# Longer latencies for five kinds of transfer in the planner of an attention and two-MLP kernel

## The chip, the core and the metric

The kernel runs on one core of a Trainium2 chip. A core has five engines that each run their own instructions in order: TensorE (PE in the profile, with PEld for its weight loads), VectorE (DVE), ScalarE (ACT), GpSimd (POOL) and SyncE (SP). SP and POOL issue the DMA transfers here. The metric is the device time of one execution in microseconds.

## The reference

Attention within chunks of 64 positions, for 8 batches, 8 heads, 576 positions and a head size of 64; its output, as 4608 tokens of 512 values, goes through two MLPs.

```python
# attention, for each chunk of 64 positions
scores = (q_c @ k_c.T) / 8.0
scores = scores - scores.max(-1)
attn = exp(scores); attn = attn / (attn.sum(-1) + 1e-9)
x = (attn @ v_c)                    # 4608 x 512
# first MLP: 512 -> 2048 -> 512
h = x @ w_in
g = maximum(h, 0) + log1p(exp(-abs(h)))
x = g @ w_out
# second MLP: 512 -> 768 -> 512
h = maximum(maximum(x @ w1, x @ w2), x @ w3)
out = h @ w_out2
```

The weights of both MLPs arrive as 64-bit floats (pairs of 32-bit words).

## The kernel before

The 4608 tokens are cut into nine blocks of 512. The first MLP's blocks 0 to 2 are multiplied plainly (L717 for x @ w_in, L737 for g @ w_out, twelve MATMULs each). Blocks 3 to 8 use a scheme with seven products of quarter matrices in place of eight: `UnitA` takes two column blocks of w_in at a time in products p1 to p7, each of six MATMULs of L1102, and `mlp1_out` (L1176) is the output step of twelve MATMULs. The second MLP does the same with `Unit2` and `Unit` (L1279, L970) and `mlp2_out` (L1387). Every f32 operand is held as a high and a low part, so each product needs three passes.

Beside the first MLP run three kinds of work that feed later stages.

- `attention(t)`: for each of 28 tiles, q, k and v are loaded into the single buffers rq, rk and rv (`loads`; L428 and L453 are the transfers), DVE transposes q and k (L623, L624), PE forms scores and the products with v of an older tile in one step (L486, tile aps), DVE and ACT do the softmax (L521 to L528), DVE transposes the result (L663), and it goes through memory and back (pd<-s at L667, s<-pd at L672).
- `early(n)`: 24 raw weights of the second MLP are loaded by POOL (L303, L308), converted from 64-bit words in six DVE steps that begin at L317 (`conv`), and stored by SP as w2d (L779) or wo2d (L774). Only one of them is under way at a time (the place kind "early").
- POOL reads prepared first-MLP weights back in each unit (s<-wac and s<-wae, L1039).

After a product PE's result in ph is copied into a tmp by ACT (`keep`, L266) or added to one by DVE (`add`, L273), and the softplus (L1124) and the cut into parts (g) follow; later products and the output step wait for those. There are nine tmps. At the end of a block `finish` copies four results from acc into tmps, and SP stores them to x2d (L705).

The order on every engine is made by `Plan.order`, before anything runs. Each operation has a cost per engine, and a latency `lat` (time behind its cost until its result can be used) or, for transfers, a `move` that occupies a modelled queue. Due times are passed back from each operation to those it depends on, less cost and latency. The planner then steps through modelled time and, on each idle engine, starts the ready operation that is due first; an operation is ready when all it depends on has ended, and the buffers that it allocates must be free. The result is one list in order of modelled start; each engine takes its own rows from it, in that order. On the chip an engine waits with semaphores wherever the modelled time was too short, and everything behind it on that engine waits too.

Of the kernel before, what the change touches and what calls it, by code (L numbers as in the profile page):

```python
# [10 lines left out]
F32 = mybir.dt.float32  # L11
# [17 lines left out]
def f32_of_bits(x):  # L29
    return float(np.array([x], np.uint32).view(np.float32)[0])  # L30
# [27 lines left out]
class Plan:  # L58
# [6 lines left out]
    def op(self, engs, fn, r=(), w=(), alloc=(), hold=(), after=(), due=None, lat=0.0, move=0.0):  # L65
        o = Op()
        o.move = move
        o.follow = o.start = None
        o.engs, o.fn, o.due, o.lat, o.allocs = engs, fn, due, lat, list(alloc)
        deps = dict.fromkeys(after)  # L70
        bufs = dict.fromkeys(o.allocs + list(hold))
        for item in r:
            b, key = item if isinstance(item, tuple) else (item, None)
            deps.update(dict.fromkeys(b.writers[key] if key in b.writers and key is not None else sum(b.writers.values(), [])))
            bufs[b] = None
        for item in w:
            b, key = item if isinstance(item, tuple) else (item, None)
            if key is None:
                deps.update(dict.fromkeys(sum(b.writers.values(), []) + sum(b.readers.values(), [])))
            else:  # L80
                deps.update(dict.fromkeys(b.writers.get(key, []) + b.readers.get(key, []) + b.readers.get(None, [])))
            bufs[b] = None
        for item in r:
            b, key = item if isinstance(item, tuple) else (item, None)
            b.readers.setdefault(key, []).append(o)
        for item in w:
            b, key = item if isinstance(item, tuple) else (item, None)
            b.writers[key] = [o]
        for b in bufs:
            if b.first is None:  # L90
                b.first = o
            else:
                deps[b.first] = None
        o.deps = list(deps)
        o.bufs = list(bufs)
        for b in o.bufs:
            b.uses += 1
        o.n = len(self.ops)
        self.ops.append(o)
        return o  # L100
# [79 lines left out]
def tile_kernel(ctx: ExitStack, tc: tile.TileContext, q, k, v, w_in, w_out, w1, w2, w3, wo2, out):  # L180
    nc = tc.nc
    B, H, S, D = q.shape
# [55 lines left out]
    wo2d = [dram.tile([P, 2, TB], F32, name=f"wo2d{j}") for j in range(NJ2)]  # L238
    w2d = [dram.tile([P, TB], F32, name=f"w2d{n}") for n in range(3 * NJ2)]
# [12 lines left out]
    def slot(*kinds, shape=[P, 2, TB], dt=F32R):  # L252
        return Buf(*kinds, fresh=lambda i: slot_at(i, shape, dt))
# [5 lines left out]
    op = plan.op  # L259
# [20 lines left out]
    NP = 3  # L280
# [9 lines left out]
    def in_line(kind, o):  # L290
        o.follow, line[kind] = line.get(kind), o
        return o


    def conv(src, view, kinds, due=None, after=(), most=("load",), rest=None, first=None, by="S"):

        raw, a, t, free = slot(*kinds, shape=[P, TB, 2], dt=I32), Buf("tmp"), Buf("tmp"), Buf(*most)
        kind, j = view

        def load(e):  # L300
            start = (nc.gpsimd if e == "G" else nc.sync).dma_start
            if kind == "in":
                start(  # L303
                    out=raw.t.rearrange("p (k f) t -> p k (f t)", k=KD),
                    in_=src[:, j * 2 * P:(j + 1) * 2 * P].rearrange("(k p) f -> p k f", p=P),
                )
            else:
                start(out=raw.t.rearrange("p f t -> p (f t)"), in_=src[j * P:(j + 1) * P, :])  # L308

        in_line("load", op({by: 0.5}, load, w=[raw], alloc=[free, raw], after=after, lat=2.0, move=2.2, due=first))  # L310
        hw = lambda: raw.t[:, :, 1]
        lw = lambda: raw.t[:, :, 0]
        ai = lambda: a.t.bitcast(I32)
        ti = lambda: t.t.bitcast(I32)
        op(
            {"D": 0.43},
            lambda e: nc.vector.tensor_scalar(ai(), hw(), 0x7FFFFFFF, None, ALU.bitwise_and),  # L317
            r=[raw],
            w=[a],
            alloc=[a, t],  # L320
        )
        op(
            {"D": 0.43},
            lambda e: nc.vector.tensor_scalar(
                a.t, a.t, f32_of_bits(0x47EFFFFF), f32_of_bits(0x38000000), ALU.min, ALU.max
            ),
            w=[a],
        )
        op(
            {"D": 0.43},  # L330
            lambda e: nc.vector.tensor_scalar(ai(), ai(), 3, 0x3FFFFFF8, ALU.logical_shift_left, ALU.bitwise_and),
            w=[a],
        )
        op(
            {"D": 0.69},
            lambda e: nc.vector.scalar_tensor_tensor(
                ai(), hw(), -0x40000000, ai(), ALU.bitwise_and, ALU.bitwise_or
            ),
            r=[raw],
            w=[a],  # L340
        )
        op({"D": 0.43}, lambda e: nc.vector.tensor_scalar(ti(), ai(), -0x800000, None, ALU.bitwise_and), r=[a], w=[t])
        last = op(
            {"D": 0.69},
            lambda e: nc.vector.scalar_tensor_tensor(
                rest.t[:, 1] if rest else t.t, lw().bitcast(U32), 2.0**-52, t.t, ALU.mult, ALU.mult
            ),
            r=[raw, t],
            w=[(rest, "rest")] if rest else [t],
            alloc=[rest] if rest else [],  # L350
            hold=[free],
            due=due,
        )
        return a, t, last
# [105 lines left out]
    def loads(fns, buf, key, move, alloc=(), engs="S", after=(), due=None):  # L460
        fns = list(fns)
        if alloc:
            op({engs: 0.0}, lambda e: None, alloc=alloc, after=after)
        for n, fn in enumerate(fns):
            op(
                {e: 0.5 if due is not None else 0.65 for e in engs},
                lambda e, fn=fn: fn({"A": nc.scalar, "S": nc.sync, "G": nc.gpsimd}[e].dma_start),
                w=[(buf, (key, n))],
                after=after,
                lat=5.0 if due is None else 1.8,  # L470
                move=move / len(fns),
                due=due,
            )
# [211 lines left out]
    def finish(b, to, due, h):  # L685

        acc = acc_of[b]
        for m in range(KD):
            o = Buf("tmp")
            src = lambda m=m: acc[m // 2].t[:, m % 2]  # L690
            if (b, m) in store:
                op(
                    {"S": 0.48},
                    lambda e, o=o, m=m: nc.sync.dma_start(out=o.t, in_=partd[b][:, m, :]),
                    w=[o],
                    alloc=[o],
                    after=[store[b, m], h],
                    lat=2.2,
                    due=due,
                )  # L700
                tt_op(lambda o=o: o.t, src, lambda o=o: o.t, ALU.add, [acc[m // 2]], [o], due=due + 4 * STEP)
            else:
                copy_op(lambda o=o: o.t, src, [acc[m // 2]], [o], psum=True, alloc=[o], due=due + 4 * STEP)
            store[b, m] = op(
                {"S": 0.48}, lambda e, o=o, m=m, to=to: nc.sync.dma_start(out=to[b][:, m, :], in_=o.t), r=[o], lat=2.5, move=1.0  # L705
            )

    def mlp1(b, j, first, last):
# [44 lines left out]
        if last:  # L753
            finish(b, partd if j < NJ - 1 else x2d, T0 + STEP * s, h)
# [5 lines left out]
    store = {}  # L760
# [7 lines left out]
    def early(n, due, after):  # L768

        if n < NJ2:  # L770
            a, t, _ = conv(wo2, ("out", n), ("x", "z"), after=after, most=("early",), by="G")
            z = slot("x", "z")
            cut_up(z, lambda: a.t, [a], alloc=[z], rest=t, due=due)
            store["o", n] = op({"S": 0.48}, lambda e: nc.sync.dma_start(out=wo2d[n], in_=z.t.bitcast(F32)), r=[z], lat=2.0, move=2.2)  # L774
            return
        n -= NJ2
        a, t, _ = conv((w1, w2, w3)[n // 2 % 3], ("in", n // 6 * 2 + n % 2), ("x", "z"), after=after, most=("early",), by="G")
        tt_op(lambda: a.t, lambda: a.t, lambda: t.t, ALU.add, [t], [a], due=due)
        store["w", n] = op({"S": 0.48}, lambda e: nc.sync.dma_start(out=w2d[n], in_=a.t), r=[a], lat=2.0, move=1.1)  # L779

    rings, first_ws = [], []

# [697 lines left out]
    for n, f in enumerate((1.0, -1.0)):  # L1480
        op(
            {"D": 0.2},
            lambda e, n=n, f=f: nc.vector.tensor_scalar(eye.t[:, n, :P], ident, f, None, ALU.mult),
            w=[(eye, n)],
            alloc=[] if n else [eye],
            after=[made],
            due=-9.0,
# [60 lines left out]
```

## Time and profile before

| | us |
|---|---|
| median of 3 runs (1430.91 to 1434.74) | 1431.5 |
| the profiled execution, its own time | 1433.25 |
| its span, first to last instruction | 1431.5 |
| PE busy | 1394.8 (97%) |
| DVE busy | 883.0 (62%) |
| ACT busy | 507.1 (35%) |
| POOL busy | 266.4 (19%) |
| mean granted TensorE clock | 0.991 |

How to read the rows further below. A table of stretches has, for each, its bounds and length, then the busy time of each engine with its instructions in brackets, the granted clock of TensorE as a share of full speed, the share of time that the DMA engines were busy, and GB/s. A timeline row has the start and length of some equal instructions that follow each other, engine, line, operation, written tile <- read tiles, shapes and count, and in square brackets the time that the engine had idled just before and what ended it. The table of waits has who waited for what: total us, number of waits, the longest. The chain of work is followed back from the last instruction; its rows have start, length and what it was. Rows of DMA issues have written <- read tile, issuing queue, count, size of one, and the median us from issue to landing. The list that orders the engines counts steps: one step of PE is a product (six MATMULs), an output step (twelve) or an attention step (64).

### The profile page before, as it was taken

The numbers are of one execution on the slowest core, as the hardware profiler recorded it, in microseconds if no ns is written. First come the engines' busy times: TensorE is split into PE (matmuls) and PEld (weight loads), VectorE is DVE, ScalarE is ACT, GpSimd is POOL, SyncE is SP. The second block draws the span as 40 slices with busy tenths as digits, with TensorE's granted clock in tenths as the row PEclk, the third lists the DMA queues.
The fourth block names the chain that finished last, engine by engine and source line by source line (L and its number), as shares of the span: only waits on it lengthen the run. The fifth ranks groups of instructions, "written<-read, shape, count | busy, mean of one in ns | idle before, by whom it ended". The sixth has DMA issues, their size and how long they took to land.

```text
span 1431.5 us, 25706 instructions
## 1 busy us (share of the span) xinstructions
PE 1394.8 (97%) x9994; PEld 1194.9 (83%) x9994; DVE 883.0 (62%) x1676; ACT 507.1 (35%) x1000; POOL 266.4 (19%) x471
## 2 busy tenths in 40 slices
PE   5999999999999999999999999999999999999998
PEld 4788878888898888888888998888888888888897
DVE  7978866858777676667664466757345444544423
ACT  3533233334344333343432445523223222322212
POOL 1000112322323323323232011111011011101300
PEclk8999999999999999999999999999999999999999
DMA  8553455775968949867476374755434533624720
GB/s 252 165 153 110 136 180 160 228 256 160 296 195 243 294 132 298 249 192 249 148 258 222 133 269 174 278 199 191 146 126 161 193 132 124 222 74 169 302 103 30
DMA packets 232474, 272.00 MB, mean 190 GB/s; under 512 B 143456, under 2 KB 163296, under 8 KB 232352
## 3 DMA queue, kind: packets, MB, share of 16 engines
q0 software_dynamic: 49472, 169.64, 33.6%
q1 hardware_dynamic: 182064, 99.93, 24.7%
q8 instruction: 79, 1.29, 0.4%
q10 hardware_dynamic: 816, 0.79, 0.2%
q14 instruction: 43, 0.35, 0.1%
HBM read 208.14 MB, written 62.13 MB: 189 GB/s over the span
## 4 chain that ended last, share of the span: by engine, by line
PE 85%; DMA 8%; DVE 3%; issue 2%; POOL 1%; SPq 1%; ACT 1%; ACTq 0%; POOLq 0%
PE ph L1279 14%; PE acc L1176 12%; PE ph L1102 12%; PE acc L1387 10%; PE one L1279 10%; PE ph L717 9%; PE acc L737 9%; DMA s<-in_moe_w_dram 2%; PE aps L486 2%; PE ph L970 2%; DMA pd<-s 2%; PE one L970 1%; PE acc L486 1%; DMA rq<-in_q_dram 1%; DMA s<-pd 1%
## 5 line engine op out<-in xcount | busy, mean ns | idle before, releaser
L1176 PE MATMUL acc<-g,s 128*128 128x512 f32 x1152 | 281.3, 393 | 0.2 <-DVE g L273 0.2
L1102 PE MATMUL ph<-s,s 128*128 128x256 f32 x2016 | 264.8, 285 | 14.4 <-DVE tmp L273 6.2
L1102 PEld LDWEIGHTS ph<-s,s 128*128 128x128 f32 x2016 | 256.6, 192 | 26.5 <-DVE tmp L273 7.6
L266 ACT COPY tmp<-ph 128x256 f32<-128x256 f32 (+1 forms) x277 | 124.9, 451 | 350.9 <-PE ph L1279 211.1
L1176 PEld LDWEIGHTS acc<-g,s 128*128 128x128 f32 x1152 | 211.9, 190 | 40.8 <-DVE g L273 0.5
L1279 PE MATMUL ph<-s,s 128*128 128x512 f32 x864 | 212.6, 389 | 0.0
L273 DVE TENSOR_TENSOR tmp<-one,tmp 128x512 f32<-128x512 f32 (+1 forms) x122 | 77.1, 632 | 211.7 <-PE one L1279 173.3
L1279 PEld LDWEIGHTS ph<-s,s 128*128 128x128 f32 x864 | 162.2, 188 | 33.6
L273 DVE TENSOR_TENSOR g<-tmp,g 128x512 fp32r<-128x512 f32 x168 | 115.3, 686 | 77.7 <-ACT g L266 77.2
L453 POOL DMA_DIRECT2D rv<-in_v_dram x152 | 93.1, 618 | 361.6 <-PE aps L486 280.4
L1279 PE MATMUL one<-s,s 128*128 128x512 f32 x648 | 158.8, 389 | 0.0
L1279 PEld LDWEIGHTS one<-s,s 128*128 128x128 f32 x648 | 121.5, 188 | 25.0
L717 PE MATMUL ph<-s,s 128*128 128x512 f32 x576 | 140.1, 393 | 0.3 <-DVE s L273 0.3
L737 PE MATMUL acc<-g,s 128*128 128x512 f32 x576 | 140.0, 392 | 0.0
L273 DVE TENSOR_TENSOR tmp<-ph,tmp 128x256 f32<-128x256 f32 (+1 forms) x172 | 76.1, 454 | 86.2 <-PE ph L1102 85.6
L717 PEld LDWEIGHTS ph<-s,s 128*128 128x128 f32 x576 | 108.7, 190 | 23.7 <-DVE s L273 0.8
L737 PEld LDWEIGHTS acc<-g,s 128*128 128x128 f32 x576 | 107.1, 188 | 22.8 <-DVE g L273 0.3
L844 POOL DMA_DIRECT2D s<-w2c x96 | 51.0, 533 | 353.4 <-PE one L1279 139.2
L266 ACT CAST g<-tmp 128x512 fp32r<-128x512 f32 x161 | 100.4, 624 | 45.7 <-PE acc L737 25.6
L1124 ACT ACTIVATE tmp<-tmp 128x256 f32<-128x256 f32 x96 | 50.4, 525 | 163.5 <-DVE tmp L273 163.5
L266 ACT CAST s<-tmp 128x512 fp32r<-128x512 f32 (+1 forms) x122 | 72.0, 599 | 48.6 <-DVE tmp L273 33.1
L1039 POOL DMA_DIRECT2D s<-wac x108 | 58.4, 542 | 158.9 <-PE ph L1102 115.4
(131 smaller groups left out, 1504.5 us busy)
## 6 DMA issues: line engine op xcount, KB each, us to landing
s<-wac POOLq DMA_DIRECT2D x108, 512.0 KB, 6.4
s<-w2c POOLq DMA_DIRECT2D x96, 512.0 KB, 4.6
w2c<-s POOLq DMA_DIRECT2D x24, 512.0 KB, 4.1
wac<-s POOLq DMA_DIRECT2D x18, 512.0 KB, 4.8
x2d<-tmp SPq DMA_DIRECT2D x36, 256.0 KB, 4.2
s<-wae POOLq DMA_DIRECT2D x18, 512.0 KB, 5.7
s<-in_moe_w_dram POOLq DMA_DIRECT2D x18, 512.0 KB, 5.8
s<-in_moe_w_in_dram SPq DMA_DIRECT2D x16, 512.0 KB, 4.4
```

The lines of the kernel that those rows point to most:

```text
L266: nc.scalar.copy(dst(), src())
L273: return op({"D": 0.69 * n}, lambda e: nc.vector.tensor_tensor(dst(), a(), b(), f), r=r, w=w, **kw)
L453: dma(out=dst().rearrange("p (c e d) -> p c e d", e=2, d=D)[half * CH:(half + 1) * CH, lo:lo + mine, h, :], in_=v[b, t % HP * 2 + h].rearr ...
L717: nc.tensor.matmul(ph.t, w[:, wi, kk * P:(kk + 1) * P], x[kk].t[:, xi], start=(kk == 0 and wi == 0 and xi == 0), stop=(kk == KD - 1 and wi ...
L737: nc.tensor.matmul(acc[m // 2].t[:, m % 2], w[:, wi, m * P:(m + 1) * P], g.t[:, gi, :], start=(first and wi == 0 and gi == 0), stop=(last ...
L844: lambda e, k=k, z=z, w=w: nc.gpsimd.dma_start(out=z.t[:, :, w].bitcast(F32), in_=(w2e[n // 2] if k == 3 else w2c[n][k])[:, :, w]),
L1039: lambda e, k=k: nc.gpsimd.dma_start(out=new[k].t.bitcast(F32), in_=wac[n][k] if k < 3 else wae[n // 2]),
L1102: nc.tensor.matmul(z.t[:, half * HT:(half + 1) * HT], ws.t[:, wi, col + kk * P:col + (kk + 1) * P], x.t[:, xi, kk * HT:(kk + 1) * HT], sta ...
L1124: in_line("y", op({"A": n}, lambda e: nc.scalar.activation(to(), src(), AF.Softplus), r=r, w=w))
L1176: nc.tensor.matmul(acc[m // 2].t[:, m % 2], w.t[:, wi, m * P:(m + 1) * P], g.t[:, gi, :], start=(first and wi == 0 and gi == 0), stop=(las ...
L1279: nc.tensor.matmul(dst(), ws.t[:, wi, col + kk * P:col + (kk + 1) * P], x[kk].t[:, xi], start=(first and kk == 0 and wi == 0 and xi == 0), ...
L1387: nc.tensor.matmul(acc[t // 2].t[:, t % 2], g.t[:, gi, t * P:(t + 1) * P], wo.t[:, wi], start=(j == 0 and wi == 0 and gi == 0), stop=(j == ...
```

## The change

Five latencies in the planner get larger; nothing that an instruction computes is touched. Raw weights that POOL loads count 9.0 in place of 2.0, the loads of q, k and v without a due time of their own (those of tiles from the second block on) 9.0 in place of 5.0, the stores of x2d at the ends of the first MLP's blocks 3 to 8 7.0 in place of 2.5, and the stores of converted weights 6.0 and 7.0 in place of 2.0.

```diff
-        in_line("load", op({by: 0.5}, load, w=[raw], alloc=[free, raw], after=after, lat=2.0, move=2.2, due=first))
+        in_line("load", op({by: 0.5}, load, w=[raw], alloc=[free, raw], after=after, lat=9.0 if by == "G" else 2.0, move=2.2, due=first))
...
-                lat=5.0 if due is None else 1.8,
+                lat=9.0 if due is None else 1.8,
...
-                {"S": 0.48}, lambda e, o=o, m=m, to=to: nc.sync.dma_start(out=to[b][:, m, :], in_=o.t), r=[o], lat=2.5, move=1.0
+                {"S": 0.48}, lambda e, o=o, m=m, to=to: nc.sync.dma_start(out=to[b][:, m, :], in_=o.t), r=[o], lat=7.0 if b >= NP else 2.5, move=1.0
...
-            store["o", n] = op({"S": 0.48}, lambda e: nc.sync.dma_start(out=wo2d[n], in_=z.t.bitcast(F32)), r=[z], lat=2.0, move=2.2)
+            store["o", n] = op({"S": 0.48}, lambda e: nc.sync.dma_start(out=wo2d[n], in_=z.t.bitcast(F32)), r=[z], lat=6.0, move=2.2)
...
-        store["w", n] = op({"S": 0.48}, lambda e: nc.sync.dma_start(out=w2d[n], in_=a.t), r=[a], lat=2.0, move=1.1)
+        store["w", n] = op({"S": 0.48}, lambda e: nc.sync.dma_start(out=w2d[n], in_=a.t), r=[a], lat=7.0, move=1.1)
```

The list that the planner makes of it differs on all engines but PE, where 984 of 991 steps keep their index and the others move by one or two. Three places.

**First piece: DVE in block 6, around one raw weight's conversion** (tile s43 before, s35 now; L317 is its first step, and the rows that read ph0 or ph1 are additions on PE's products). Before:

```order
L273 TENSOR_TENSOR g2_74<-tmp2_77,g2_74 128x512
L317 TENSOR_SCALAR tmp6_81<-s43_314_7291 128x512
L324 TENSOR_SCALAR tmp6_81<-tmp6_81 128x512
L331 TENSOR_SCALAR tmp6_81<-tmp6_81 128x512
L273 TENSOR_TENSOR tmp4_79<-ph1_90,tmp4_79 128x256
L336 SCALAR_TENSOR_TENSOR tmp6_81<-s43_314_7291,tmp6_81 128x512
L342 TENSOR_SCALAR tmp0_75<-tmp6_81 128x512
L345 SCALAR_TENSOR_TENSOR tmp0_75<-s43_314_7291,tmp0_75 128x512
L273 TENSOR_TENSOR tmp6_81<-tmp6_81,tmp0_75 128x512
L273 TENSOR_TENSOR g0_72<-tmp4_79,g0_72 128x512
L273 TENSOR_TENSOR tmp5_80<-ph1_90,tmp5_80 128x256
```

And now:

```order
L273 TENSOR_TENSOR g2_74<-tmp5_80,g2_74 128x512
L273 TENSOR_TENSOR tmp2_77<-ph1_90,tmp2_77 128x256
L273 TENSOR_TENSOR g0_72<-tmp2_77,g0_72 128x512
L273 TENSOR_TENSOR tmp0_75<-ph1_90,tmp0_75 128x256
L623 STREAM_TRANSPOSE s41_319_7428<-rq0_71 128x512
L317 TENSOR_SCALAR tmp4_79<-s35_316_7327 128x512
L273 TENSOR_TENSOR tmp8_83<-ph1_90,tmp8_83 128x256
L324 TENSOR_SCALAR tmp4_79<-tmp4_79 128x512
L273 TENSOR_TENSOR g1_73<-tmp0_75,g1_73 128x512
L331 TENSOR_SCALAR tmp4_79<-tmp4_79 128x512
```

L317 stood ahead of the two additions on ph1 behind g2; now both stand ahead of it, with the g0 between them.

**Second piece: POOL at the start of block 7, around the load of another raw weight** (L303; the other rows read prepared weights back). Before:

```order
L1039 DMA s7_341_7956<-wac2_1_127 128x1024
L1039 DMA s27_342_7959<-wae1_145 128x1024
L1039 DMA s28_344_7993<-wac3_0_129 128x1024
L303 DMA s43_345_8034<-in_moe2_w2_dram 128x4x256
L1039 DMA s18_346_8044<-wac3_2_131 128x1024
L1039 DMA s9_347_8062<-wac3_1_130 128x1024
```

And now:

```order
L1039 DMA s21_341_7956<-wac2_1_127 128x1024
L1039 DMA s19_342_7959<-wae1_145 128x1024
L303 DMA s34_343_7977<-in_moe2_w2_dram 128x4x256
L1039 DMA s27_345_7996<-wac3_0_129 128x1024
L1039 DMA s4_346_8042<-wac3_2_131 128x1024
L1039 DMA s9_347_8061<-wac3_1_130 128x1024
```

The load stands one row earlier and goes into buffer s34 in place of s43; on DVE its L317 stands behind the same rows as before.

**Third piece: SP and ACT at the end of block 3**, where four results leave through x2d (its tmps are 7, 3, 2 and 5 before, 2, 3, 8 and 1 now). SP before:

```order
L428 DMA rk0_84<-in_k_dram 32x4x32 x4
L705 DMA x2d3_183<-tmp7_82 128x512
L428 DMA rq0_71<-in_q_dram 32x12x32
L672 DMA s45_214_4894<-pd0_87 32x2x256 x4
L428 DMA rq0_71<-in_q_dram 32x12x32 x3
L428 DMA rq0_71<-in_q_dram 32x4x32 x4
L705 DMA x2d3_183<-tmp3_78 128x512
L428 DMA rk0_84<-in_k_dram 32x12x32 x4
L428 DMA rk0_84<-in_k_dram 32x4x32 x4
L705 DMA x2d3_183<-tmp2_77 128x512
L705 DMA x2d3_183<-tmp5_80 128x512
```

SP now:

```order
L705 DMA x2d3_183<-tmp2_77 128x512
L667 DMA pd0_87<-s41_216_4936 128x512
L428 DMA rk0_84<-in_k_dram 32x12x32
L672 DMA s45_210_4856<-pd1_88 32x2x256 x4
L428 DMA rk0_84<-in_k_dram 32x12x32 x3
L428 DMA rk0_84<-in_k_dram 32x4x32 x4
L705 DMA x2d3_183<-tmp3_78 128x512
L705 DMA x2d3_183<-tmp8_83 128x512
L705 DMA x2d3_183<-tmp1_76 128x512
```

ACT some rows behind the copies of that block end, before:

```order
L266 COPY s7_211_4835<-aps0_91 128x512
L266 CAST g1_73<-tmp8_83 128x512
L266 COPY tmp7_82<-ph0_89 128x256
L525 ACTIVATE p0_86<-p0_86,drop_235 128x512
L266 COPY tmp3_78<-ph1_90 128x256
L1124 ACTIVATE tmp7_82<-tmp7_82 128x256
```

And now:

```order
L266 CAST g1_73<-tmp6_81 128x512
L266 COPY tmp2_77<-ph0_89 128x256
L266 COPY s35_209_4827<-aps0_91 128x512
L525 ACTIVATE p0_86<-p0_86,drop_235 128x512
L266 COPY tmp0_75<-ph1_90 128x256
L1124 ACTIVATE tmp2_77<-tmp2_77 128x256
```

On SP the last three stores stand in a row and behind a write of pd and four reads of it; on ACT the COPY behind L525 goes to tmp0 where it went to tmp3.

## Rows read from the trace of the kernel before

**Rows 1.** Table of stretches that make up the span, all engines.

```profile
0.00:40.00 40.00, 24.82 (x716) 20.11 (x717) 32.42 (x73) 15.92 (x27) 4.51 (x13) 0.80 0.84 246
40.00:320.00 280.00, 278.02 (x2208) 226.43 (x2207) 209.53 (x418) 98.95 (x172) 41.93 (x72) 1.00 0.59 174
320.00:760.00 440.00, 425.38 (x3700) 379.68 (x3699) 301.02 (x601) 174.51 (x383) 131.50 (x222) 0.99 0.74 228
760.00:1431.50 671.50, 666.55 (x3374) 568.69 (x3374) 340.04 (x585) 217.75 (x419) 88.47 (x164) 1.00 0.48 168
```

**Rows 2.** Timeline of PE, rows with idle time ahead, 320 to 760 us.

```profile
348.41 2.42 PE L1102 MATMUL ph<-s,s 128*128 128x256 f32 x18 [0.52 <-ACT tmp L1124]
...
382.48 0.97 PE L1102 MATMUL ph<-s,s 128*128 128x256 f32 x6 [0.51 <-ACT tmp L1124]
...
393.62 0.98 PE L1102 MATMUL ph<-s,s 128*128 128x256 f32 x6 [1.81 <-ACT tmp L266]
463.47 0.98 PE L1102 MATMUL ph<-s,s 128*128 128x256 f32 x6 [2.54 <-ACT tmp L266]
505.51 2.93 PE L1102 MATMUL ph<-s,s 128*128 128x256 f32 x12 [2.04 <-DVE tmp L273]
...
758.11 0.97 PE L1102 MATMUL ph<-s,s 128*128 128x256 f32 x6 [0.55 <-ACT tmp L1124]
```

**Rows 3.** Table of DVE's waits, 340 to 770 us, those at L317.

```profile
DVE tmp L317 <- DMA s<-in_moe_w_dram: 41.2, 16, 5.2
...
DVE tmp L317 <- DMA s<-in_moe_w_out_dram: 8.6, 3, 3.9
```

**Rows 4.** Timeline of DVE and POOL, around two of L317's waits.

```profile
475.62 0.43 DVE L317 TENSOR_SCALAR tmp<-s 128x512 int32<-128x512 int32 x1 [2.77 <-DMA s<-in_moe_w_dram]
...
654.43 0.76 POOL L303 DMA_DIRECT2D s<-in_moe_w_dram  x1 [0.20 <-issue]
...
662.72 0.43 DVE L317 TENSOR_SCALAR tmp<-s 128x512 int32<-128x512 int32 x1 [4.62 <-DMA s<-in_moe_w_dram]
...
663.99 0.42 DVE L273 TENSOR_TENSOR tmp<-ph,tmp 128x256 f32<-128x256 f32 x1
```

**Rows 5.** Timeline of SP's queue and of ACT, end of block 3.

```profile
456.47 0.62 SPq L705 DMA_DIRECT2D x2d<-tmp  x1
...
463.04 0.37 ACT L266 COPY tmp<-ph 128x256 f32<-128x256 f32 x1 [5.58 <-DMA x2d<-tmp]
```

**Rows 6.** Table of stretches, around PE's two longest waits.

```profile
462.00:472.00 10.00, 8.53 (x42) 7.37 (x43) 6.87 (x14) 3.13 (x8) 3.67 (x6) 0.83 0.87 263
498.00:512.00 14.00, 11.96 (x120) 10.64 (x119) 7.87 (x15) 4.09 (x9) 5.38 (x9) 0.88 0.85 264
```

**Rows 7.** Chain of work that ended last, 464 to 600 us.

```profile
464.44 4.34 PE acc L1176 x12
...
470.94 2.75 PE acc L1176 x12
473.68 2.87 PE ph L1102 x24
...
480.01 1.09 PE aps L486 x64
...
505.51 2.93 PE ph L1102 x12
...
598.72 1.70 PE ph L1102 x12
```

**Rows 8.** DMA issues of raw weights by POOL; L303's times to landing (SP's too).

```profile
s<-in_moe_w_dram POOLq DMA_DIRECT2D x18, 512.0 KB, 5.8
...
s<-in_moe_w_out_dram POOLq DMA_DIRECT2D x6, 512.0 KB, 5.5
...
DMA to landing us min/median/max: 3.7/5.4/9.3
```

**Rows 9.** Timeline of POOL, start of block 7.

```profile
724.50 0.77 POOL L303 DMA_DIRECT2D s<-in_moe_w_dram  x1 [5.49 <-PE ph L1102]
```

## The prediction

> **What bounds the kernel now.** I read the stretches of the span first: there the reader sees where TensorE (PE) has time to give. Of 1431.5 us PE is busy 1394.78. The idle rest is 15.2 us in the first 40 us, 2.0 up to 320 us, 14.6 (440.00 less 425.38) from 320 to 760 us and 5.0 behind that, which is the tail after the last MATMUL [rows 1]. So PE is the bound everywhere, and the later part of the first MLP up to 760 us is the one stretch where an edit of the plan's order can win. The start lies ahead of everything that the change moves, and the tail holds only the last stores.
>
> Next, PE's own rows in that stretch, with the idle time before each. There are sixteen, from 348.41 to 758.11 us; six are shown [rows 2]. PE waits in them for a DVE or ACT result in tmp. To see why those were late I took DVE's waits: it stood 41.2 + 8.6 = 49.8 us at L317, the first step of a raw weight's conversion, 19 times, for the weight's DMA [rows 3]. One place in full [rows 4]: POOL issues the weight at 654.43, DVE stands 4.62 us for it, starts L317 at 662.72, and only at 663.99 takes the addition on ph that stands three rows behind. PE stalls 0.6 to 0.7 us twice behind that. Thirteen of the sixteen stalls follow a wait at L317 in this way: the first is the one at 382.48, the last at 758.11, and they sum to 11.2 us. One, 2.54 us at 463.47, has another cause: ACT's COPY into a tmp waits 5.58 us for the store of x2d out of it, which SP issued at 456.47 [rows 5]. The first (0.52) and a small one behind it (0.17) come ahead of these waits and stay in the sum as they are.
>
> The stalls cost more than their idle time. Around the two longest the granted clock is 0.83 and 0.88, a mixture of the levels 1.2 and 2.4 GHz, though PE had been busy until 2.54 and 2.04 us before [rows 6]. Behind the first, twelve MATMULs of L1176 take 4.34 us in place of 2.75; behind the second, twelve of L1102 take 2.93 in place of 1.70 [rows 7]. That is 1.59 + 1.23 us.
>
> **Part by part.** No instruction is added or taken away; 24 copies change between DVE and ACT (0.7 against 0.6 us, beside PE work). PE keeps its sequence: 984 of its 991 steps stand at the same index, the rest moves by one or two. What moves is where DVE, POOL and SP put their work beside it.
>
> *Raw weights by POOL (lat 2.0 to 9.0), 24 loads.* The planner writes one list, from which each engine takes its rows, so I counted the PE steps that the list has between a load's issue and its L317, and priced them by the trace: a product of six MATMULs 0.72 us (2.87 for four), an output step 2.75, an attention step 1.09 [rows 7]. Before, there are 4.9 to 8.4 us of PE work between (median 6.0); now 7.4 to 12.0 (median 9.8). The loads take 5.8 and 5.5 us from issue to landing as medians and up to 9.3 [rows 8], so the first range is too short and the second mostly enough. For the load of rows 4: four products and an output step before, 4 x 0.72 + 2.75 = 5.6 us; six products, an output step and an attention step now, 8.2 us. Its wait of 4.62 shrinks by 2.5 to 2.1 us. Doing that for each of the 19 waits leaves 6.7 of the 49.8 us, never more than 2.3 in one place. In the trace a wait of 2.77 us at 475.62 cost PE nothing [rows 4]: its next stall is the one at 505.51 [rows 2]. Larger waits cost 0.51 to 2.04. So of the stalls of this cause I leave 1.2 us (two of the small size), and 11.2 - 1.2 + 1.23 for the clock = 11.2 us go. Between the ends (nothing goes, or 12.4 us) this is near the upper, because 43 of the 49.8 us of waiting are covered by counted PE work.
>
> Where the load itself moves, it passes others on POOL: in the second piece of order it goes ahead of one s<-wac. Its own issue, 0.77 us, delays that one, and at the same time its buffer is another, so that the 5.49 us that POOL stood in front of it at 724.50 [rows 9] need not come again. The s<-wac transfers are hidden: the list has at least 16 us of PE work between any of them and its first MATMUL, which is more than any landing of [rows 8], and no PE row waits for one. Zero, and up to that cover.
>
> A rule speaks against this part. The trace shows 5.5 to 5.8 us for these 512 KB. The Trainium skill, page "DMA: Bandwidth & Descriptors", section "Anatomy of one DMA — SWDGE (gpsimd) path", gives such a transfer a fixed 2.0 us plus its bytes at 436 GB/s, which makes an estimate of 3.2 us. By that price the old plan's allowance was ample, and the sum would hold only the next item. The rows disagree with it on this queue under this load.
>
> *Stores (x2d 2.5 to 7.0, w2d and wo2d to 6.0 and 7.0).* The plan now thinks a tmp occupied until about when it is free. In the third piece of order the COPY that waited writes tmp0, which no store of this block end reads, in place of tmp3, and the three late stores stand together. At the block ends up to 760 us every tmp is next taken at least 13 us of PE work behind its copy in the list, before 5.7. The 2.54 us go, with the 1.59 of the clock: 4.1. Bounds: nothing, if another wait is just behind, and the whole.
>
> *q, k, v (5.0 to 9.0).* The buffers rq, rk, rv are single, so most of these loads can't be asked for sooner; in the list they even stand some 5 us of PE work later, and their L623 and L624 some 8 later. What is late next would be the attention step on PE. The list keeps at least 20 us between L624 and that step behind 320 us, and 4.9 in the worst case before (9.2 until now). No PE row in 320 to 760 us waits at L486. I take zero; ends are a gain of 0 and a loss that is a rival below.
>
> *What comes in their place.* Conversions now land among other urgent DVE work; the smallest margin of the g that the output step reads shrinks in the list by about 0.5 us. Nearest row: the 0.52 us stall that no load caused [rows 2]. I take two of these, 1.0 us; ends 0 and the 2.0 us of idle time that 40 to 320 us shows without any such load.
>
> Sum: 11.2 + 4.1 - 1.0 = 14.3, taken as 14.5 since the 2.0 us before 320 can also shrink. Behind 760 us PE never idles until the tail and its sequence is the same, so what is won stays won. The profiled execution took 1433.25 us, 1.75 more than its span; it lies that much above the median of 1431.5. So 1418.75 for it, and **1417.0** for the median.
>
> **Rivals.**
> 1. *Still late.* POOL gets to a load later than the list says (it idles 5.49 us in front of one), and half of the L317 stalls remain. For it: that row. Against: the waits measured include this delay already. 11.2 halves: 1422.6.
> 2. *The page's price holds* and the waits at L317 had another cause than the length of the transfers: only the stores win, 1431.5 - 4.1 = 1427.4. Against: each wait ends with that DMA.
> 3. *The wait moves to the attention step.* L623 and L624 come later; if PE waits 0.5 us at each of the 28 steps behind the change, 14 us come back: 1431.0. For: the margin of 9.2 falls to 4.9. Against: no such row now, and 20 us of cover in most.
> 4. *Slower: SP blocks the block ends.* SP runs in order. In the third piece a write pd<-s and reads s<-pd now stand ahead of the three x2d stores. If DVE's L663 comes more than some 6 us late there (13 us of cover less 6.6 us from the issue of the store at 456.47 to the end of the wait [rows 5]), tmps stay taken and ACT blocks as at 463.04, at each of six block ends: 6 x 4.1 us. With the L317 gain kept: 1431.5 - 10.2 + 24.8 = 1446. For: it is what one of six block ends shows now. Against: the cover doubled.
>
> **How the numbers follow.** Forecast 0.66, rivals 0.14, 0.02, 0.10, 0.08. About 0.3% (4.3 us) is what a measurement of this kernel can tell from no change. Faster: forecast and rival 1, 0.80; within it rivals 2 and 3, 0.12; slower rival 4, 0.08. The most there is to win is 14.6 + 2.8 + 2.0 = 19.4 us, which makes the low end 1412. The high end takes in rivals 1 and 2: 1428; beyond lie 0.18.
>
> **What would show it.** Right: L317's two rows of DVE's waits fall from 49.8 to under 10 us; PE is busy over 437 of the 440 us that follow 320; the granted clock there is 1.00 in every slice; ACT's wait for x2d is gone; the stretch behind 760 us is as long as before. Wrong: stalls of PE on L486 (rival 3), ACT waiting for x2d at several block ends (rival 4), L317 waits over 20 us (rival 1), or L317 waits gone with PE's idle time unchanged, which would mean that DVE's standing was not what held PE.

## Result and the profile after

The changed kernel takes 1417.0 us (median of 5 runs, 1412.2 to 1420.8) against 1431.3: a ratio of 0.9896, 95% interval 0.9871 to 0.9922. Run a second time beside the later experiments it took 1416.3 against 1432.9 (0.9882, 0.9859 to 0.9906). The profiled execution, 1417.03 us, has a span of 1415.2.

The table of stretches of the changed kernel, all engines (columns as in [rows 1]; the last row is the surroundings of PE's one long stall, as [rows 6]):

```profile
0.00:40.00 40.00, 24.92 (x717) 20.42 (x718) 32.28 (x72) 15.91 (x27) 4.53 (x13) 0.83 0.85 248
40.00:320.00 280.00, 278.02 (x2228) 226.30 (x2229) 211.24 (x422) 98.80 (x172) 41.82 (x72) 1.00 0.58 169
320.00:760.00 440.00, 436.71 (x3794) 392.84 (x3787) 309.25 (x613) 179.94 (x393) 136.47 (x231) 1.00 0.77 238
760.00:1415.20 655.20, 650.57 (x3275) 554.18 (x3273) 333.52 (x573) 211.44 (x407) 83.20 (x155) 1.00 0.47 167
376.00:386.00 10.00, 7.23 (x36) 6.08 (x34) 5.23 (x9) 2.36 (x6) 1.05 (x2) 0.83 1.05 319
```

From 320 to 760 us PE is idle 440.00 - 436.71 = 3.3 us where it was 14.6 [rows 1]. The start (15.1) and the rest behind 760 us (655.20 - 650.57 = 4.6) are as they were. The timeline of PE from 320 to 1300 us has two rows with idle time left, of sixteen [rows 2]:

```profile
347.72 2.42 PE L1102 MATMUL ph<-s,s 128*128 128x256 f32 x18 [0.52 <-ACT tmp L1124]
380.13 1.14 PE L1102 MATMUL ph<-s,s 128*128 128x256 f32 x6 [2.77 <-ACT tmp L266]
```

The first is the one that no load causes. The second is new. Of DVE's waits, 340 to 780 us, there are left at L317 and at the two steps that read q and k, L623 and L624 (total, times, longest; [rows 3] had 41.2 and 8.6 us for L317):

```profile
DVE s L624 <- issue: 4.0, 2, 3.7
...
DVE s L623 <- PE aps L486: 1.9, 3, 0.7
...
DVE s L623 <- DMA s<-pd: 1.2, 3, 0.6
...
DVE tmp L317 <- DMA s<-in_moe_w_dram: 0.9, 2, 0.5
...
DVE s L624 <- DMA rk<-in_k_dram: 0.2, 1, 0.2
```

The profile infers who ended a wait, and "issue" is where it names nobody. The long one of these is a wait for k all the same: DVE stands 3.66 us ahead of L624 at 376.87, the last load of k before it was issued at 368.7, and the loads of k there took up to 8.0 us to land.

The loads did not get shorter; the list of DMA issues, which answers [rows 8], shows them longer, and DVE stands for them only 0.9 us in all:

```profile
s<-in_moe_w_dram POOLq DMA_DIRECT2D x18, 512.0 KB, 6.8
...
s<-in_moe_w_out_dram POOLq DMA_DIRECT2D x6, 512.0 KB, 6.3
```

What the new stall is, the chain of waits shows (start, length, what), and with it ACT's row from the timeline:

```profile
369.99 9.12 DMA wo2d<-s
...
380.13 1.14 PE ph L1102 x6
381.28 4.17 PE acc L1176 x12
...
388.88 2.75 PE acc L1176 x12
```

```profile
379.19 0.62 ACT L266 CAST s<-tmp 128x512 fp32r<-128x512 f32 x1 [5.54 <-DMA wo2d<-s]
```

ACT is to write a slot (one of the buffers named s) out of which SP stores wo2d; the store took 9.12 us, ACT stood for 5.54, and the COPY that stands behind it on ACT was late for PE. Behind the stall twelve MATMULs of L1176 take 4.17 us in place of 2.75, at a granted clock of 0.83 in the 10 us around it.

### The profile page after: what moved, and what is told of

Same layout as the page of the kernel before. It is cut to its first block, busy times and chain, and to the rows that moved or that the text cites. A ratio compares the mean times of both kernels' runs of the same rounds, so it can differ in the third digit from the quotient of the medians.

```text
span 1415.2 us, 25698 instructions
## 1 busy us (share of the span) xinstructions
PE 1390.2 (98%) x9994; PEld 1193.7 (84%) x9994; DVE 886.3 (63%) x1678; ACT 506.1 (36%) x998; POOL 266.0 (19%) x471
## 4 chain that ended last, share of the span: by engine, by line
PE 96%; DMA 1%; DVE 1%; ACT 1%; issue 0%; SPq 0%; ACTq 0%
PE acc L1176 18%; PE ph L1102 17%; PE ph L1279 14%; PE acc L1387 10%; PE one L1279 10%; PE acc L737 9%; PE ph L717 9%; PE aps L486 3%; PE ph L970 2%; PE one L970 1%; PE acc L486 1%; PE ph L388 1%; DMA wo2d<-s 1%; PE ph L389 1%; DMA rk<-in_k_dram 1%; ACT s L266 0%
## 5 line engine op out<-in xcount | busy, mean ns | idle before, releaser
L1176 PE MATMUL acc<-g,s 128*128 128x512 f32 x1152 | 280.7, 393 | 0.0
L1176 PEld LDWEIGHTS acc<-g,s 128*128 128x128 f32 x1152 | 211.5, 189 | 40.3
```

Of the source, the lines that this page charges most:

```text
L1176: nc.tensor.matmul(acc[m // 2].t[:, m % 2], w.t[:, wi, m * P:(m + 1) * P], g.t[:, gi, :], start=(first and wi == 0 and gi == 0), stop=(las ...
```

## Experiments

Each run is compared with the kernel before on its own chip. "Stalls" is PE's idle time from 320 to 760 us. The next three are from DVE's waits, 340 to 780 us: "L317" for raw weights, "q, k" those at L623 and L624 that the profile puts to loads of q or k, and "all" everything that DVE waited ahead of L623 and L624, whoever is named. Since the names are inferred, "all" is the safer of the two. These four are of one profiled execution each, the times of several; the whole change and e9, which are one kernel, show how far one execution can be from another.

| kernel | median us | ratio (95%) | stalls | L317 | q, k | all |
|---|---|---|---|---|---|---|
| before | 1431.3 | | 14.6 | 49.8 | 3.0 | 6.5 |
| whole change | 1417.0 | 0.9896 (0.9871-0.9922) | 3.3 | 0.9 | 0.2 | 7.3 |
| e1 raw weights alone | 1424.1 | 0.9942 (0.9920-0.9964) | 10.7 | 0 | 12.1 | 21.7 |
| e2 x2d alone | 1431.6 | 1.0008 (0.9990-1.0025) | 13.8 | 49.8 | 5.4 | 7.9 |
| e3 q, k, v alone | 1432.9 | 1.0012 (0.9995-1.0029) | 16.2 | 49.2 | 0.7 | 5.4 |
| e4 whole without q, k, v | 1421.2 | 0.9926 (0.9901-0.9951) | 5.9 | 0.8 | 11.3 | 19.4 |
| e5 whole without x2d | 1420.2 | 0.9926 (0.9906-0.9946) | 5.4 | 1.3 | 4.5 | 7.2 |
| e6 whole, wo2d 12 | 1416.9 | 0.9911 (0.9888-0.9934) | 4.5 | 0.2 | 10.2 | 13.0 |
| e7 whole, raw 12 | 1413.0 | 0.9874 (0.9855-0.9894) | 0.5 | 0 | 0.7 | 2.5 |
| e8 before, half the bytes | 1420.6 | 0.9933 (0.9915-0.9952) | 4.7 | 32.9 | 0 | 6.0 |
| e9 whole change again | 1416.3 | 0.9882 (0.9859-0.9906) | 5.0 | 5.0 | 1.3 | 6.6 |
| e10 whole, raw 12 again | 1413.2 | 0.9859 (0.9834-0.9884) | 0.5 | 0 | 1.4 | 2.3 |
| e11 whole, raw 15 | 1413.8 | 0.9866 (0.9842-0.9889) | 0.5 | 0 | 0 | 6.0 |
| e12 whole, raw 5 | 1431.3 | 0.9986 (0.9970-1.0002) | 12.9 | 31.7 | 0 | 2.3 |

The w2d and wo2d allowances have no run of their own: set alone, they leave the planner's order on every engine as it was before and give two operations another buffer. What they are worth within the change is not shown.

### The parts one by one

**e1**, the first line of the change and nothing else:

```diff
-        in_line("load", op({by: 0.5}, load, ..., lat=2.0, move=2.2, due=first))
+        in_line("load", op({by: 0.5}, load, ..., lat=9.0 if by == "G" else 2.0, move=2.2, due=first))
```

> Only the allowance of POOL's raw-weight loads goes from 2 to 9; the stores and q, k, v stay as before. In the list the PE work between such a load's issue and its L317 has a median of 9.8 us (before 6.0), and by the same sum 5.9 of the 49.8 us of waits at L317 stay. Theory (the loads are the main cause, the parts add up): about 10.2 to 11.2 us less than before, 1420 to 1421; L317's waits under 8 us; the wait of ACT's COPY for x2d (5.6 us) stays, with its PE stall of 2.5 us. Rival (the waits at L317 had another cause than the length of the transfers): within 2 us of before. Rival (the gain comes only with the later q, k, v loads, which now stand out of the way): at most half, 1426 or more.

It came to 0.9942, about 7 to 8 us where 10 to 11 were expected. L317's waits for raw weights are gone to the last, and yet PE stands 10.7 us. The timelines of PE and, in the second fence, of DVE show why for the two longest stalls:

```profile
490.44 3.47 PE L1102 MATMUL ph<-s,s 128*128 128x256 f32 x18 [2.89 <-ACT tmp L1124]
...
583.91 2.42 PE L1102 MATMUL ph<-s,s 128*128 128x256 f32 x18 [2.11 <-ACT tmp L1124]
```

```profile
488.05 0.71 DVE L624 STREAM_TRANSPOSE s<-rk 128x512 f32<-128x512 f32 x1 [2.79 <-DMA rk<-in_k_dram]
...
489.25 0.41 DVE L273 TENSOR_TENSOR tmp<-ph,tmp 128x256 f32<-128x256 f32 x1
...
580.31 0.71 DVE L624 STREAM_TRANSPOSE s<-rk 128x512 f32<-128x512 f32 x1 [3.30 <-DMA rk<-in_k_dram]
...
582.44 0.42 DVE L273 TENSOR_TENSOR tmp<-ph,tmp 128x256 f32<-128x256 f32 x1
```

It is the same picture as in [rows 4] with another load in it. DVE, no longer held at L317, comes to L624 before k has landed, stands 2.79 and 3.30 us, and takes the addition on ph that PE's next tmp hangs on 1.2 and 2.1 us after it starts there; PE stalls 2.89 and 2.11 us. In the kernel before, the wait at L317 hid that q and k are late: DVE's waits for them grow from 3.0 to 12.1 us, and all its waits ahead of L623 and L624 from 6.5 to 21.7.

These two stalls are 5.0 of the 10.7 us. A third, 1.36 us at 471.35, follows 4.24 us of waiting ahead of L624. Two more follow stores: 2.03 us at 361.09, where L317 stands 2.70 us for a tmp out of which x2d is being stored, and 1.33 us at 482.39, where ACT stands 4.96 us for a wo2d store. The stall of 2.54 us behind ACT's wait for x2d, which was expected to stay, did not come. So the wait for raw weights hid late stores as well as late q and k.

**e2**, x2d alone:

```diff
-                ..., r=[o], lat=2.5, move=1.0
+                ..., r=[o], lat=7.0 if b >= NP else 2.5, move=1.0
```

> Only the allowance of the x2d stores goes from 2.5 to 7. In the order ten rows of DVE, seven of ACT and three of POOL move, none of PE or SP. Theory (parts add up): the 2.54 us stall of PE at 463 goes, with 1.6 us of slow clock behind it: 4.1 us less, 1427. Rival (that time only pushes PE into the next late result): within 1.5 us of before, 1430 to 1431, and the stall at 505 grows.

Nothing, as the rival had it, but not at the place that it named: the stall at 505 shrank to 1.38 us. The stall at 463 is gone, and in its place stand three in the next 20 us (PE, then the row of DVE from which the last two come):

```profile
467.10 2.41 PE L1102 MATMUL ph<-s,s 128*128 128x256 f32 x18 [0.76 <-ACT tmp L1124]
479.34 0.98 PE L1102 MATMUL ph<-s,s 128*128 128x256 f32 x6 [1.46 <-ACT tmp L1124]
482.40 1.70 PE L1102 MATMUL ph<-s,s 128*128 128x256 f32 x12 [1.00 <-DVE tmp L273]
```

```profile
477.34 0.43 DVE L317 TENSOR_SCALAR tmp<-s 128x512 int32<-128x512 int32 x1 [4.46 <-DMA s<-in_moe_w_dram]
```

The wait at L317 that cost nothing at 475.62 [rows 4], because PE had stood 2.54 us just before, is 4.46 us long now and costs 2.5. A stall gives the loads behind it time; taken away alone, it is paid at the next one.

**e3**, q, k, v alone, and **e4**, the whole change without them:

```diff
-                lat=5.0 if due is None else 1.8,
+                lat=9.0 if due is None else 1.8,
```

> Only the allowance of the q, k, v loads goes from 5 to 9. Theory: no gain by itself, 1431. Since DVE's and POOL's rows move with it, the PE work between a raw weight's issue and its L317 falls from 6.0 to 5.6 us (median), by which the waits at L317 grow from 49.8 to about 59 us and PE loses about 2 us: 1433. Rival (later q, k, v loads free SP and the transfers beside them, so that the raw weights land sooner): L317's waits shrink by a third, 1427. Rival 3 of the prediction (the wait moves to the attention step L486): PE stalls on L486, 1440 or more.

> The whole change but for q, k, v, whose allowance stays at 5. The PE work between issue and L317 is as in the whole change (median 9.8 us). Theory (q, k, v count for nothing): as the whole change, 1415 to 1419. Rival (the gain needs q, k, v out of the way): 1424 or more.

Alone the part is worth nothing (1.0012, with 1 in the interval), and L317's waits did not grow to 59 us. Within the change it is worth about 4 us: 1421.2 without it, 0.9926 against 0.9896 and 0.9882. That lies between e4's theory (up to 1419) and its rival (1424 or more), and the intervals overlap. DVE's waits of e4 look like those of e1 again:

```profile
DVE s L624 <- DMA rk<-in_k_dram: 6.8, 3, 2.9
DVE s L623 <- DMA rk<-in_k_dram: 4.5, 2, 3.8
```

All of DVE's waits ahead of L623 and L624 are 19.4 us in e4, and 7.3 and 6.6 in the two profiles of the whole change. So the later L623 and L624 are what keeps DVE from standing for q and k, once it no longer stands for raw weights; not wholly, as the 3.66 us at 376.87 show.

**e5**, the whole change without x2d's line (the diff of e2 undone):

> The whole change but for the x2d stores, whose allowance stays at 2.5. The order differs from the whole change in eleven rows of DVE, five of ACT and three of POOL. Alone the x2d part gained nothing, since PE ran on into the next late result. Theory (with those gone it gains, as the parts need each other): one stall of 2 to 3 us at the end of a block, ACT's COPY standing for x2d again, and slow clock behind it: 3 to 4 us over the whole change, 1420 to 1421. Rival (the x2d part is worth nothing): as the whole change, 1417.

As the theory had it. PE and ACT's waits (340 to 780 us):

```profile
378.60 0.98 PE L1102 MATMUL ph<-s,s 128*128 128x256 f32 x6 [2.11 <-ACT tmp L266]
450.13 0.98 PE L1102 MATMUL ph<-s,s 128*128 128x256 f32 x6 [2.72 <-ACT tmp L266]
```

```profile
ACT tmp L266 <- DMA x2d<-tmp: 8.2, 2, 5.6
```

The stall at the end of block 3 is back (2.72 us at 450.13, ACT standing 5.6 us for x2d). The part that gains nothing alone gains 3 to 4 us once DVE no longer stands for raw weights, though here too the intervals overlap.

### Is it the length of the transfers?

**e8** keeps the kernel before with its order and shortens the transfers themselves:

```diff
-                    out=raw.t.rearrange("p (k f) t -> p k (f t)", k=KD),
...
+                    out=raw.t.rearrange("p (k f) t -> p k (f t)", k=KD)[:, :KD // 2 if by == "G" else KD],
...
-        hw = lambda: raw.t[:, :, 1]
...
+        half = by == "G"
...
+        word = lambda x, i: x[:, None, :TB // 2, i].to_broadcast([P, 2, TB // 2]) if half else x[:, :, i]
+        hw = lambda: word(raw.t, 1)
...
```

> The kernel before, with its own allowances and its own order on every engine; POOL's 24 raw-weight loads bring only half of each weight (256 KB), and the conversion reads that half twice, so that all other work stays and the result is another. Theory (the waits at L317 come from the transfers' length): landing falls from 5.8 to about 4 us, the 49.8 us of waits at L317 to under 20, and the time by more than half of what the allowance alone gave: 1424 to 1427. Rival (POOL issues late, or DVE stands for its queue and not for the bytes): waits over 40 us and 1430 or more.

The issues of DMAs, DVE's waits (its L321 is L317 of the others) and the stretch of 320 to 760 us:

```profile
s<-in_moe_w_dram POOLq DMA_DIRECT2D x18, 256.0 KB, 4.9
s<-in_moe_w_out_dram POOLq DMA_DIRECT2D x6, 256.0 KB, 4.4
```

```profile
DVE tmp L321 <- DMA s<-in_moe_w_dram: 26.1, 13, 3.7
DVE tmp L321 <- DMA s<-in_moe_w_out_dram: 6.8, 2, 3.5
```

```profile
320.00:760.00 440.00, 435.33 (x3742) 390.35 (x3733) 308.91 (x617) 178.44 (x391) 137.28 (x232) 1.00 0.74 223
```

Landing falls by only 0.9 to 1.1 us, the waits by 17 us and not by the 30 expected, and the time by more than expected: 0.9933, nearly 10 us. With no allowance touched, shorter transfers give back about 60% of what the change gained; the rival falls. Not all of it need be L317's: ACT's longest wait for x2d fell too, from 5.58 [rows 5] to 2.6 us, and the stall at 463 is gone; how much that gave is not shown. The run also shows that the loss doesn't follow the sum of the waits: 32.9 us of waits, none over 3.7, leave stalls of 4.7 us.

**e12**, 5 for the raw weights within the whole change, is the counterpart:

> 5 for POOL's raw-weight loads, the rest of the change as it is: the PE work between issue and L317 stays at a median of 5.6 us, under the 5.8 us that the loads take, though the allowance has more than doubled. Theory (what counts is the work that stands between, not the number): L317's waits stay at 40 to 50 us, and only the stores' gain remains, 1428. Rival (later q, k, v loads let the weights land sooner): L317's waits under 25 us, 1422 or less.

```profile
DVE tmp L317 <- DMA s<-in_moe_w_dram: 23.8, 13, 5.5
DVE tmp L317 <- DMA s<-in_moe_w_out_dram: 7.9, 3, 3.9
```

```profile
661.48 2.93 PE L1102 MATMUL ph<-s,s 128*128 128x256 f32 x12 [4.21 <-DVE tmp L273]
```

These are DVE's waits and PE's longest stall. 31.7 us of waits, as many as in e8, but the longest 5.5 us, and stalls of 12.9 us. The time is that of before (0.9986), though all other parts of the change and a larger allowance are in it. The allowance is less far from the old one than 5 from 2: `Plan.order` also books a load on its modelled queue, which lets it end 1.0 + 2.2 + 0.8 = 4.0 us behind its issue at the earliest, so the old 2.0 counted as 4.0, where 5 makes 0.5 + 5.0 = 5.5 and 9 makes 9.5. So what counts is the PE work that the list puts between issue and L317 (a median of 5.6 us here, 6.0 before, 9.8 in the change), as the theory had it; the waits were smaller than its 40 to 50, and the stores' gain of 3 us did not show.

### What is left, and a faster version

**e6** was to take away the stall at 380 us:

```diff
-            store["o", n] = op(..., lat=6.0, move=2.2)
+            store["o", n] = op(..., lat=12.0, move=2.2)
```

> The whole change with the allowance of the wo2d stores at 12 in place of 6. In the profile of the whole change one stall is left that the start of the first MLP does not show before it: 2.77 us at 380.13, where ACT's CAST into a slot stands 5.54 us for a wo2d store out of it, which took 9.1 us. In the list the PE work between such a store and the next use of its slot is now 11.6 us or more (5.6 to 13.3 with 6). Theory (that store is what is left): the stall goes with the 1 to 1.5 us of slow clock behind it, 4 us under the whole change: 1413. Rival (the order moves in 128 rows of DVE and 35 of ACT, and another operand is late in its place): 1417 or more.

The stall went, and the time is the rival's: 1416.9. PE and DVE:

```profile
564.16 2.93 PE L1102 MATMUL ph<-s,s 128*128 128x256 f32 x12 [3.98 <-DVE tmp L273]
```

```profile
563.08 0.71 DVE L624 STREAM_TRANSPOSE s<-rk 128x512 f32<-128x512 f32 x1 [5.48 <-DMA rq<-in_q_dram]
```

128 rows of DVE moved with that one number, and L624 stands 5.48 us somewhere else.

**e7**, **e10** and **e11** give the raw weights more, 12 (twice) and 15:

```diff
-        in_line("load", op({by: 0.5}, load, ..., lat=9.0 if by == "G" else 2.0, move=2.2, due=first))
+        in_line("load", op({by: 0.5}, load, ..., lat=12.0 if by == "G" else 2.0, move=2.2, due=first))
```

> The whole change with 12 in place of 9 for POOL's raw-weight loads: the median of the PE work between issue and L317 is 12.3 us (9.8 with 9), and a raw weight holds its slot 2.5 us longer. Theory (9 covers what the transfers take, up to 9.3 us): L317's waits are near nothing in both, no gain, 1415 to 1420. Rival (held slots delay others: ACT or POOL waits for a slot's store): 1422 or more. Rival (what is left of stalls comes from loads still late): 1413.

> The whole change once more, beside the next three on one chip: 1415 to 1419, with one late stall of 2 to 3 us where a store out of a slot is waited for.

> The whole change with 12 for POOL's raw-weight loads, once more. Its first profile had no stall of PE between 320 and 760 us but the 0.52 us that no load causes. Theory (the difference to the whole change is real): 1413, some 4 us under the whole change of the same chip. Rival (chance of one chip): within 1.5 us of it.

> 15 for POOL's raw-weight loads: the PE work between issue and L317 has a median of 15.6 us, and 385 rows of DVE and 99 of ACT stand otherwise than in the whole change. Theory (with the transfers covered, nothing is left to win): as with 12, 1413. Rival (weights held longer take slots and POOL's time from s<-wac): 1417 or more, with waits of POOL or ACT for slots.

12 is some 3 us faster than the change: 1413.2 beside 1416.3 on one chip (e10, e9), where the intervals overlap, and 1413.0 on another (e7). The eight times with 12 lie from 1410.2 to 1414.1, the ten of the whole change from 1412.2 to 1420.8. In its timeline of PE one row with idle time is left between 320 and 820 us; the first fence is e7, the second e10:

```profile
320.00:760.00 440.00, 439.48 (x3824) 395.44 (x3823) 303.52 (x606) 180.99 (x396) 137.21 (x231) 1.00 0.77 236
...
349.14 2.42 PE L1102 MATMUL ph<-s,s 128*128 128x256 f32 x18 [0.52 <-ACT tmp L1124]
```

```profile
345.31 2.42 PE L1102 MATMUL ph<-s,s 128*128 128x256 f32 x18 [0.52 <-ACT tmp L1124]
```

Two things went. With 9 raw weights were still late in places, as e7's second rival had it: L317 waited 0.9 us in one profile of the whole change and 5.0 in the other (e9), where PE's stall of 1.46 us at 589.59 follows 2.06 us of waiting at L317 for a load that took 9.4 us to land. With 12 it waited not at all. The wait for the wo2d store (a stall of 2.77 us, and 2.57 in e9) is gone as well, in another order. 15 does no harm that the times show; its PE waits have one new row, an operand of rv that ACT copies late:

```profile
PE ph L1279 <- ACT rv L266: 1.3, 1, 1.3
```

But for that 0.5 us these versions have nothing left to win between 320 and 760 us.

## Why the prediction was right

The time forecast was 1417.0 and it is 1417.0; that close, it is also luck, since terms were off on both sides and cancelled. To set them against the runs I take out the start, which varies: e7 and e10 are one kernel, and the row with 0.52 us of idle time stands at 349.14 in one and at 345.31 in the other. Behind that row to the end of the span there are 1412.3 - 349.14 = 1063.2 and 1408.4 - 345.31 = 1063.1 us in these two (no stall left), 1431.5 - 348.41 = 1083.1 before, 1415.2 - 347.72 = 1067.5 with the change.

- **What bounds it, and the most there is to win: right.** PE was the bound, the stretch of 320 to 760 us the only place, and what is won there stayed won to the end. The whole of the stalls is worth 1083.1 - 1063.2 = 19.9 us. The 0.2 us added for the stretch ahead of 320 did not come: it has 2.0 us of idle time as before.
- **A term was missing.** Of these 19.9 us, 13.95 are the idle time of the fifteen later stalls and 2.8 the clock. The other 3.1 us are 0.2 for each stall. The rows that come near it are the products of six behind a stall, which take 0.97 or 0.98 us [rows 2] in place of 0.72 [rows 7]. They were shown; the sum left them out.
- **Raw weights: right in cause, cover and place.** Left over were 6.7 us of waits by the count of PE work; 0.9 and 5.0 were measured. e8 and e12 show that it is the length of the transfers against that work. But the step from waits to stalls, all 11.2 us from this part, was too much for it alone: e1 gained 7 to 8 us, since late q, k and stores stalled PE in place of the weights.
- **q, k, v, "I take zero": wrong.** The step looked for what is late next on PE, at L486, and nothing waits there behind 320 us in any run. What is late next is DVE itself at L624 (e1, e4). With the wait at L317 gone and the q, k, v part missing, about 4 us stay (e4). The later place of L623 and L624, booked as a risk, is the gain.
- **Stores, 4.1 us: right in size, wrong as a sum of parts.** x2d is worth 3 to 4 us within the change (e5) and nothing alone (e2). The stall that the 4.1 us were read from did not come in e1, where x2d's allowance was as before, so that its size fits is partly luck. No run has the w2d and wo2d allowances apart.
- **What comes in their place, 1.0 us: too small.** 1067.5 - 1063.2 = 4.3 us: the stall of 2.77 at 380.13 and its clock, 4.17 - 2.75 = 1.4; e9 has a further 1.9 us of stalls. It is a kind that the prediction priced only for x2d: rival 4 had SP's stores late at the block ends, and it was a store of wo2d, which the change meant to cover.
- **Rivals.** "Still late" falls with L317's 0.9 and 5.0 us, "the wait moves to the attention step" with no row at L486, "SP blocks the block ends" with no wait of ACT for x2d (its 24.8 should be 6 x 4.1 = 24.6; nothing hangs on it). "The page's price holds" falls with e1 and e8. The price is that of the Trainium skill, page "DMA: Bandwidth & Descriptors", section "Anatomy of one DMA — SWDGE (gpsimd) path". From its 436 GB/s, 256 KB fewer are 0.6 us as an estimate, and the trace is near it with 0.9 for L303's loads and 1.1 for L308's. Its fixed 2.0 us the trace doesn't bear out under this load: a line through 4.9 and 5.8 us leaves 4.0.
- **Signs.** L317 under 10 us: 0.9. PE busy over 437 of 440 us: 436.7, just missed. The clock at 1.00 in every slice: no, 0.83 around 380 us. ACT without a wait for x2d: yes. The time behind 760 us: as before.

## To carry to other kernels

Where an engine that works in order stands for one load, it hides whatever else is late on it: before you book a wait as gain, look for the next operand on that same engine whose load was issued no sooner, not only at the engine that bounds the kernel. The parts of such a change don't add up (alone they gave 7 to 8, 0 and 0 us, the w2d and wo2d stores not tried alone, together 14 to 17), so they are tried together and taken out one at a time. An allowance near the longest landing can still be too small, because the work that the planner puts under a load scatters: with 9 there were 7.4 to 12.0 us of it, the loads landed in up to 8.3 and 9.4 us (L303's in the two profiles), and some still came late. 12 left none late. And each new allowance makes a new order, in which another operand can be late (e6), so the profile is read again for each.

## What the runs showed of the hardware

- Half the bytes of a load by POOL's queue saved 0.9 of 5.8 us. The same 512 KB took 5.8 us as a median before, 6.8 with the change and 5.7 in e7, so from one version of the kernel to another the landing moved by as much as with half the size. What moved it is not shown.
- How long PE has stood doesn't tell alone whether the clock falls. The granted clock was 0.83 to 0.88, as a mean of 10 to 14 us, around stalls of 2.04 and 2.54 us [rows 6] and of 2.77, and 1.00 around one of 2.86 us in e3 and one of 2.72 in e5 (rows of stretches around them, e3 first):

```profile
482.00:494.00 12.00, 10.20 (x63) 9.22 (x64) 10.74 (x24) 4.05 (x9) 7.30 (x12) 1.00 0.88 229
```

```profile
448.00:460.00 12.00, 9.87 (x113) 8.68 (x114) 7.38 (x14) 4.70 (x11) 4.69 (x8) 1.00 0.85 255
```

- One kernel, e7 and e10, took 3.8 us longer up to its first stall at some 350 us in one profiled execution than in the other, and 0.1 us longer behind it: nearly all that these two differ by.
